# V's weights loaded later, and a scan whose odd bank is given back and written back by ScalarE

## The chip, the cores and the metric

The kernel runs on one core of one Trainium2 chip. The core has TensorE (matrix products into PSUM, eight banks of 512 fp32 columns on 128 partitions), VectorE, ScalarE and GpSimd (elementwise work), and SyncE, here only an issuer of DMA transfers; ScalarE and GpSimd can issue transfers as well. The engines run side by side, each takes its own instructions in program order, and semaphores order them among each other. In the profile PE is TensorE (PEld its weight loads), DVE VectorE, ACT ScalarE, POOL GpSimd, SP SyncE; a q behind a name (SPq, ACTq) means the engine's issues of DMA transfers.

The metric is device time in microseconds of the whole kernel, the median of several runs.

## The reference

Two independent heads over 2048 tokens of width 448; their outputs lie side by side, 896 columns in bf16.

```python
# head A: a diagonal complex state-space scan over all tokens
Lam_bar = exp(dt * Lam);  B_bar = ((Lam_bar - 1) / Lam)[:, None] * Bmat
Bu = x @ B_bar.T                       # complex, 448 states
h[t] = Lam_bar * h[t-1] + Bu[t]
yA = 2 * Re(h @ Cmat.T) + x * Dskip
# head B: local dilated attention, 16 heads of width 28
q, k, v = split(x @ wqkv)
# token s looks at s, s-2, ..., s-14 (8 keys, masked before the start)
yB = (softmax(q . k / sqrt(28)) @ v) @ wo
out = concatenate([yA, yB], axis=-1)
```

## The kernel before

Every piece of work is a unit: a Python closure with the engine that runs it, its dependencies and the PSUM banks that it takes and gives back. `Planner.run` (line 162) emits the units in the order of one hand-kept list of unit numbers, `ORDER` (line 46), and `BANKS` (line 76) says which banks each taking of a slot gets. So the order on every engine and on every queue is fixed by that list; a number from 1000 on means the second engine of a unit that has two to choose from. The costs and priorities written beside the units do not act at run time.

Head B. `loads` (line 322) brings B_x transposed, on SP, into the tile `rb`: the first 1024 tokens in four transfers (line 348), the others in four (line 352). The Q and K columns of `wqkv` come in three groups of columns, the first on ScalarE's queue, the others on SP's (line 359), and are copied between the partition halves by `shift` (line 381, seen as line 201 on ScalarE and 205 on VectorE). `load_v` (line 391) brings V's columns into `wv` in four transfers, lines 336 to 340. `prep` (line 427) projects Q and K: `first` (line 485, matmuls of line 493) for two key tiles of the first 1024 tokens, `proj` (line 438, line 452) for the rest; evictions are copies of line 201 and 203 into `qk`. `dup` (line 531) copies the last key tile to the other partition half with SP. `qk` (line 538) multiplies Q with shifted K on VectorE (line 559) and sums over head columns on TensorE (line 572). `softmax` (line 587), `v_proj` (line 655, matmuls of line 672 reading `wv`) and `pv` (line 709) follow: VectorE multiplies weights with V (line 726), adds (732) and folds (735 to 743), SP turns the folded sums (line 770), TensorE applies `wo` (lines 789 and 796), and copies into `ra` go out by line 806.

Head A. A_x is loaded transposed, sixteen transfers of line 867 and one of 870, into `xaT_sb`. The scan (line 1093) treats 16 consecutive tokens as 4 by 4 steps, and goes over 7 groups of 64 states. In each group TensorE forms the inputs of four steps (line 1134) in banks: "P" holds steps 0 and 2 (two banks), "1" and "3" one each. ScalarE reads "P" into `eP` (line 1147), TensorE adds powers of it to "1" and "3" (line 1151), ScalarE reads "1" into `e1` (line 1155), and so on through "3", a two-level chain of small copies and products over all 128 blocks (lines 1173, 1178, 1184); then `ev3` (line 1187) writes step 3, `s5` (line 1202, matmuls of 1190 and 1191) adds the carry to "1" and `ev1f` reads step 1; `s6` and `s7` do the same for "P", and `evPf` reads steps 0 and 2. What happens to a bank between the first reading and the carry is in `FIN`, for "P" and "1" in this order:

```python
FIN = (("seed", "hold"),) * 7
```

"hold" keeps the bank with its sums until the carry is added; "seed" gives it back after the reading and later takes a bank again, into which ScalarE copies the read sums (line 1216 for "P"; `back1`, line 1195, would do it for "1"). `powers` (line 1067) makes the matrices of powers, on VectorE (line 1083) or ScalarE (line 1081).

`outputs` (line 1308) multiplies the states by C (line 1318) for pairs of tokens, adds x times Dskip (matmuls of 1337 for half of the tokens, a ScalarE copy of line 1330 into the bank for the others), copies the sums into `ra` (line 201 on ScalarE, 205 on VectorE) and sends them out on SP (line 1341). The last three pairs are copied and sent one token at a time.

Of the kernel before, what the change touches and what calls it, by code (L numbers as in the profile page):

```python
# [9 lines left out]
ACT = mybir.ActivationFunctionType  # L10
# [6 lines left out]
D = 448  # L17
# [22 lines left out]
NHO = 4  # L40
NF = 3
WARM = (7, 4)
FIN = (("seed", "hold"),) * 7
PES = (0, 1)
PRI = dict(bm=-5.66, xa=2.77, cc=19.9, sc=2.9, ch=-27.35, bk=-0.56, v0=16.0, v1=-26.16, wo=-13.74, y=14.16, pw=-5.68, sm=13.48, lim=100.0, lim2=30.0, limv=70.0, qk=0.86, K11=-14.0, Q11=-13.0, K10=-12.0, Q10=-11.0, K01=-10.0, Q01=-9.0, K00=-8.0, Q00=-7.0, d3=10.94, h0=-1.0, g0=-1.0, h1=-1.0, g1=-1.0, h2=-1.0, g2=-1.0, h3=1.0, g3=-1.0, h4=-1.0, g4=-1.0, h5=-1.0, g5=-1.0, h6=1.0, g6=1.0, nd=4.0, xd=20.12)
ORDER = [
# [28 lines left out]
]  # L75
BANKS = [
    0, 0, 2, 3, 5, 0, 2, 4, 6, 2, 4, 0, 6, 4, 2, 0, 2, 4, 0, 2, 4, 0, 4, 6, 7, 0, 2, 6, 0, 7, 6, 2, 0, 1, 2, 4,
    5, 2, 5, 4, 7, 5, 2, 2, 5, 3, 2, 0, 0, 6, 5, 4, 6, 0, 3, 2, 6, 0, 6, 0, 1, 6, 4, 6, 4, 2, 6, 2, 0, 2, 6, 0,
    4, 2, 6, 0, 4, 2,
]  # L80
TWO_PI = 2.0 * math.pi
MAGIC = 12582912.0
# [2 lines left out]
def pe(n, cols):  # L85
    return n * (cols / 2400.0 + 0.003)


def act(n):
    return n / 1200.0 + 0.055  # L90


def vec(n):
    return n / 960.0 + 0.07
# [26 lines left out]
class Planner:  # L121
# [6 lines left out]
    def add(self, eng, cost, fn, deps=(), prio=0.0, acq=None, rel=None, lat=None, until=None,  # L128
            mode="f", kind=None, dma=0.0):
        u = Unit()  # L130
        u.mode, u.kind, u.dma = mode, kind, dma
        u.eng = eng if isinstance(eng, tuple) else (eng,)
        u.cost = cost if isinstance(cost, tuple) else (cost,)
        u.fn, u.prio, u.until = fn, prio, until
        u.acq, u.rel = [() if v is None else tuple(v) if isinstance(v, (tuple, list)) else (v,) for v in (acq, rel)]
        u.lat = {"PE": 0.275, "ACT": 0.22, "DVE": 0.27}.get(u.eng[0], 0.15) if lat is None else lat
        u.deps = [d for d in deps if d is not None]
        u.end, u.seq, u.on = None, len(self.units), None
        self.units.append(u)
        return u  # L140
# [171 lines left out]
class PartB:  # L312
# [396 lines left out]
    def pv(self, b, prio, deps):  # L709
# [8 lines left out]
        for r in range(2):  # L718
# [27 lines left out]
            for x in (0, 1):  # L746
                o = 4 * r + 8 * x
                dd = [self.u_vh[b, p] if p < HALO else self.u_v[b, p - HALO] for p in range(o, o + 10)]
                ms.append(P.add("DVE", vec2(4 * n1), lambda x=x, f=mul: f(x), [*dd, *after, last], prio + 0.1 * r))
            last = P.add("DVE", vec2(4 * n1) + 0.11, add, ms, prio + 0.1 * r)  # L750
            if g < 3:
                last = P.add("DVE", vec2(2 * n1) + vec2(n1) + 0.2, fold, [last, *self.u_proj, self.u_trd.get(g - 2)], prio + 0.1 * r)
# [71 lines left out]
class PartA:  # L824
# [268 lines left out]
    def scan(self, prio, qk_done):  # L1093
# [8 lines left out]
        for m in range(NM):  # L1102
# [8 lines left out]
            def hget(m=m):  # L1111
                if m not in self.h:
# [7 lines left out]
            sl = {"P": Slot("B", 2, 0, 2), 1: Slot("B", 2), 3: Slot("B", 2), "fl": Slot("fl"),  # L1120
                  "P2": Slot("B", 2, 2 if FIN[m][0] == "seed" else 0, 2), "b1": Slot("B", 2, 2 if FIN[m][1] == "seed" else 0)}
            begun = set()
# [69 lines left out]

            mP, m1 = FIN[m]

# [113 lines left out]
    def outputs(self, prio):  # L1308
        nc, pool, P, cx = self.nc, self.pool, self.plan, self.cx
        for n, j in enumerate(range(0, T, 2)):  # L1310
            pr = prio + n / 100
            jb = {}
# [5 lines left out]
                    nc.tensor.matmul(ps, lhsT=self.h[m][:, i, g * NCH:(g + 1) * NCH], rhs=self.Ccat[:, m, :],  # L1318
                                     start=False, stop=(m == NM - 1), skip_group_check=True)

            def ev(eng, j=j, jb=jb, j0=0, j1=2):
                cx.late_tile()
                if j0 == 0:
                    jb["r"] = cx.ya_ring.get()
                o = cx.ya_v[:, jb["r"], j0:j1]
                cx.copy(eng, o, jb["y"][:, j0:j1, 0:D])

            def seed(j=j, jb=jb):
                jb["y"] = self.psum.tile([NCH, 2, 512], f32, name="y_ps", slot=jb["s"])
# [14 lines left out]
            sl = jb["s"] = Slot("B", 1, 0 if j // 4 in PES else 1, 2)  # L1344
            pc = pe(7, 448)
            hs = [self.u_h[:20], self.u_h[20:24], self.u_h[24:]]
            if j // 4 in PES:
                first = [P.add("PE", pe(4, 112), lambda f=skip, i=i: f(i), [self.u_dg, self.u_x[j], self.u_x[j + 1], *self.u_xx.values()],
                               pr, acq=sl) for i in range(2)]
# [3 lines left out]
            if n < 3:  # L1353
                pc -= pe(2, 448)
                us = [P.add("PE", pc, lambda f=y, i=i: f(i, m1=5), hs[0] + self.u_cc + first, pr, acq=sl) for i in range(2)]
                v = P.add("PE", pe(2, 448), lambda f=y: (f(0, m0=5, m1=6), f(1, m0=5, m1=6)), us + hs[1], pr)
                v = P.add("PE", pe(2, 448), lambda f=y: (f(0, m0=6), f(1, m0=6)), [v] + hs[2], pr)
                us = [v, v]
            else:
                us = [P.add("PE", pc, lambda f=y, i=i: f(i), self.u_h + self.u_cc + first, pr, acq=sl) for i in range(2)]  # L1360
            en = lambda n: (("ACT", "DVE"), (act(n) + 0.13 * (n > 512), vec(n)))
            e = lambda f, **k: (lambda eng: f(eng, **k))
            if n < 5:
                v = P.add(*en(896), e(ev), us + x + cx.u_free, pr - 2, rel=sl, acq="ya")
                P.add("SP", 0.45, out, [v], pr, rel="ya", lat=1.1, dma=1.0)
            else:
                u = P.add(*en(448), e(ev, j0=0, j1=1), us[:1] + x + cx.u_free, pr - 2, acq="ya")
                o = P.add("SP", 0.45, lambda f=out: f(j0=0, j1=1), [u], pr, lat=1.1, dma=0.5)
                v = P.add(*en(448), e(ev, j0=1, j1=2), [us[1], u], pr - 2, rel=sl)
                P.add("SP", 0.45, lambda f=out: f(j0=1, j1=2), [v, o], pr, rel="ya", lat=1.1, dma=0.5)  # L1370


@with_exitstack
def kernel(
# [36 lines left out]
    cx = Ctx(tc, pool, _Ps(), plan)  # L1411
    cx.dram = ctx.enter_context(tc.tile_pool(name="dram", bufs=1, space=bass.MemoryType.DRAM))
    b = PartB(cx, B_x, B_wqkv, B_wo, out[0].rearrange("(b p j) e -> b p j e", b=2, j=JB)[:, :, :, D:2 * D])
# [14 lines left out]
    cx.consts2()  # L1428
    b.prep(u_warm)
    a.load_x([b.u0])  # L1430
    b.load_v([b.u0])
    a.setup_weights(PRI["bm"])
    cx.u_bm = a.u_bm
    b.load_wo(a.u_bm)
# [42 lines left out]
```

## Time and profile before

| | us |
|---|---|
| three runs | 137.06, 136.56, 135.93 (median 136.56) |
| the profiled execution | 136.07 |
| its span, first to last instruction | 134.4 |
| TensorE busy in the span | 126.9 |
| VectorE busy | 113.8 |
| ScalarE busy | 103.4 |
| mean granted TensorE clock | 1.00 |

The profile is that of one execution. Busy time is the time in which an engine had at least one instruction running; matmuls are pipelined and their ends are modelled, so a busy TensorE can still wait. The chain that ended last is followed back from the last instruction: at each step to what released it, or to the instruction before it on its engine. A row of a timeline gives the start, the duration, the engine, the line, what is written from what, and in brackets how long the engine stood idle before it and what ended that. A row of a group gives line, engine, operation, output from input, shapes, count, then busy microseconds, mean nanoseconds of one, and idle time before.

### The profile page before, as it was taken

To read this page: it belongs to the slowest core of one execution; us is meant where nothing else is said; L and a number is where in the kernel's file an instruction comes from. 1 tells how busy PE (TensorE), PEld (TensorE's weight loads), DVE (VectorE), ACT (ScalarE), POOL (GpSimd) and SP (SyncE) were. 2 spreads that over 40 slices of the span, in tenths; PEclk is the share of its full clock that TensorE was granted. 3 is DMA by queue.
4 is the path that set the end of the run, shared out by engine and by line. 5 is a ranking of instruction groups with operands and counts; after the bars stand their busy time and mean duration, and the time that the engine had idled before them with its cause. 6 is when DMAs were issued, how large, how long until landed. Compare 5 with 4: busy or idle time off the path is not lost.

```text
span 134.4 us, 2479 instructions
## 1 busy us (share of the span) xinstructions
PE 126.9 (94%) x921; PEld 63.5 (47%) x921; DVE 113.8 (85%) x131; ACT 103.4 (77%) x189; POOL 9.7 (7%) x28
## 2 busy tenths in 40 slices
PE   6968999999999999999999899999999999999990
PEld 2445544433546344564544445454556555455440
DVE  5215999999999999999999999999999999991120
ACT  2027999999899987797789998988979737877141
POOL 6940070000000000000000000000000000000000
PEclk9999999999999999999999999999999999999999
DMA  4999999473854749855558989125810630459543
GB/s 101 238 270 225 170 165 211 104 151 84 92 124 99 197 95 282 207 122 126 148 129 137 242 211 250 61 67 138 231 49 0 153 121 0 143 172 262 187 145 120
DMA packets 47759, 20.25 MB, mean 151 GB/s; under 512 B 38774, under 2 KB 46346, under 8 KB 47748
## 3 DMA queue, kind: packets, MB, share of 16 engines
q1 hardware_dynamic: 45716, 18.96, 61.6%
q10 hardware_dynamic: 1840, 1.11, 3.3%
q8 instruction: 7, 0.11, 0.3%
q0 software_dynamic: 192, 0.03, 0.1%
q14 instruction: 4, 0.03, 0.1%
HBM read 5.18 MB, written 4.19 MB: 70 GB/s over the span
## 4 chain that ended last, share of the span: by engine, by line
PE 82%; ACT 6%; DMA 4%; SPq 4%; issue 1%; ACTq 0%
PE banks L1318 15%; PE banks L1134 15%; PE banks L452 12%; PE banks L672 8%; PE banks L789 7%; PE banks L572 6%; DMA rb<-in_B_x_dram 4%; PE banks L1178 3%; SPq L348 3%; PE banks L493 2%; PE banks L1151 2%; PE banks L796 2%; PE banks L1191 2%; ACT eP L1147 1%; ACT pbuf L1173 1%
## 5 line engine op out<-in xcount | busy, mean ns | idle before, releaser
L559 DVE TENSOR_TENSOR prods<-qk 128x4096 bf16<-128x4096 bf16 (+1 forms) x18 | 31.8, 1810 | 0.2
L1134 PE MATMUL banks<-xaT_sb,Bcat 128*128 128x512 bf16 (+1 forms) x112 | 26.7, 382 | 0.0
L201 ACT CAST ra<-banks 128x896 bf16<-128x896 f32 (+2 forms) x22 | 16.9, 802 | 8.6 <-PE banks L1318 5.2
L201 ACT CAST qk<-banks 128x512 bf16<-128x512 f32 (+3 forms) x20 | 16.9, 846 | 1.6 <-PE banks L1191 1.2
L732 DVE TENSOR_TENSOR prods<-prods 128x7168 bf16<-128x7168 bf16 x4 | 15.6, 3891 | 0.1
L726 DVE TENSOR_TENSOR prods<-ra 128x7168 bf16<-128x7168 bf16 x4 | 15.5, 3886 | 0.1
L726 DVE TENSOR_TENSOR prods<-ra,qk 128x7168 bf16<-128x7168 bf16 x4 | 15.5, 3886 | 0.0
L1318 PE MATMUL banks<-Ccat,h 128*128 128x448 bf16 x64 | 14.8, 354 | 0.0
L452 PE MATMUL banks<-rb 128*128 128x512 bf16 (+1 forms) x64 | 14.0, 380 | 0.0
L1134 PEld LDWEIGHTS <-Bcat 128*128 128x128 bf16 (+1 forms) x112 | 9.0, 100 | 10.5 <-issue 4.0
L672 PE MATMUL banks<-wv,rb 128*128 128x448 bf16 (+1 forms) x64 | 13.4, 354 | 0.0
L1173 ACT CAST pbuf<-banks 128x64 bf16<-128x64 f32 (+1 forms) x42 | 9.5, 233 | 3.8 <-PE banks L1178 2.9
L1318 PE MATMUL banks<-Ccat,qk 128*128 128x448 bf16 x48 | 11.7, 352 | 0.0
L789 PE MATMUL banks<-wo_p,rb 128*128 128x448 bf16 x48 | 10.5, 354 | 0.0
L1178 PE MATMUL banks<-pbuf,pw 128*128 128x64 bf16 x77 | 10.1, 235 | 0.3 <-ACT pbuf L1173 0.3
L493 PE MATMUL banks<-rb 128*128 128x256 bf16 (+2 forms) x76 | 7.9, 256 | 1.8 <-DMA rb<-in_B_x_dram 0.6
L1178 PEld LDWEIGHTS <-pw 128*128 128x128 bf16 x77 | 6.4, 105 | 5.9 <-issue 1.6
L203 ACT ACTIVATE qk<-banks 128x512 bf16<-128x512 f32 (+2 forms) x10 | 8.5, 850 | 0.2
L1318 PEld LDWEIGHTS <-h 128*128 128x128 bf16 x64 | 5.9, 99 | 5.5 <-issue 0.9
L452 PEld LDWEIGHTS <-rb 128*128 128x128 bf16 (+1 forms) x64 | 5.0, 97 | 7.1 <-issue 2.5
L1147 ACT CAST eP<-banks 128x1024 bf16<-128x1024 f32 x7 | 7.2, 1023 | 1.5 <-PE banks L1134 1.5
L201 ACT CAST h<-banks 128x512 bf16<-128x512 f32 (+1 forms) x8 | 6.5, 808 | 1.9 <-PE banks L1191 1.8
(145 smaller groups left out, 191.8 us busy)
## 6 DMA issues: line engine op xcount, KB each, us to landing
out_dram<-ra SPq DMA_DIRECT2D x12, 224.0 KB, 2.4
xaT_sb<-in_A_x_dram SPq DMA_DIRECT2D x2, 448.0 KB, 4.1
out_dram<-ra SPq DMA_DIRECT2D x8, 112.0 KB, 1.7
ra<-ra SPq DMA_DIRECT2D x2, 392.0 KB, 4.4
qk<-qk SPq DMA_DIRECT2D x2, 392.0 KB, 3.7
wv<-in_B_wqkv_dram ACTq DMA_DIRECT2D x2, 336.0 KB, 5.2
ra<-ra SPq DMA_DIRECT2D x1, 588.0 KB
qk<-qk SPq DMA_DIRECT2D x1, 588.0 KB, 5.0
```

The costliest lines, as they stand in the source:

```text
L201: nc.scalar.copy(out, in_)
L452: nc.tensor.matmul(out(e)[:, j0:j1], lhsT=w, rhs=self.xB[rows, b, j0:j1, c, :], start=e not in begun, stop=True, skip_group_check=True)
L493: nc.tensor.matmul(box["ps"][:, e, k, 64 * j0:64 * j1], lhsT=self.wqk[rows, c, D * k + NCH * kt:D * k + NCH * kt + NCH], rhs=self.xB[rows, ...
L559: V.tensor_tensor(p[:, :, a:a + n], q[:, t0 + a:t0 + a + n].unsqueeze(1).to_broadcast([NCH, 4, n]), bass.AP(k.tensor, k.offset, [k.ap[0], ...
L672: nc.tensor.matmul(box["ps"][:, e, 0:D], lhsT=self.xB[rows, b, jj, c, :], rhs=self.wv[rows, c, :], start=e not in begun, stop=True, skip_g ...
L726: V.tensor_tensor(out.rearrange("p (u i d h) -> p u i d h", u=4, i=4, d=DH), self.attn[b][:, r].rearrange("p (x u i) h -> p x u i h", x=2, ...
L732: V.tensor_tensor(T1, T1, T2, op=ALU.add)
L789: nc.tensor.matmul(ps, lhsT=o[:, kt + x, :], rhs=self.wo_p[:, (KT + 1) * x + kt, :], start=(kt == 0), stop=False, skip_group_check=True)
L1134: mt(ps(i), lhsT=lhsT, rhs=rhs, start=i not in begun, stop=True, **kw)
L1173: nc.scalar.copy(pb[:, dst, PAD:PAD + NCH // d], tot(a, d))
L1178: mt(tot(out, 2), lhsT=L(T * unit * k), rhs=pb[:, src, PAD - sh:PAD - sh + NCH // 2], start=False, stop=True, **kw)
L1318: nc.tensor.matmul(ps, lhsT=self.h[m][:, i, g * NCH:(g + 1) * NCH], rhs=self.Ccat[:, m, :], start=False, stop=(m == NM - 1), skip_group_ch ...
```

## The change

1. V's weights: the unit of `load_v` depends on the eviction of the third key tile of the first 1024 tokens in place of the start marker, and the order runs it on SP, after all B_x loads, seven A_x loads, the load of B and the first `dup`. Before, it was run on ScalarE's queue at the start.
2. The scan: "1" is treated as "seed" too. Its bank is given back after `ev1`, and `back1` on ScalarE (a copy of 128x512 from `e1` into a newly taken bank) comes in for each of the seven groups, seven new units.
3. The last output pair: the copy of its second token is cut in two, columns 0 to 255 on ScalarE and 256 to 447 on VectorE, and the bank is given back after the transfer.
4. The numbers in `ORDER` and `BANKS` are new throughout. What changes in substance: A_x's loads come in another order (the load of B stands after the first three of them, the second `dup` after the last); the first powers of group 0 are made on VectorE, no longer on ScalarE; one of the copies of the first softmax weights goes from VectorE to ScalarE; TensorE's sequence of scan products, V projections and output products is of the same kind with many neighbours exchanged; the last TensorE units are the second tokens of pairs 12 and 14, before it was 10 and 12. The constants in `Planner.add` differ, but act on nothing at run time.

```diff
-FIN = (("seed", "hold"),) * 7
+FIN = (("seed", "seed"),) * 7
 ORDER = [
-    0, 1, 23, 3, 2, 5, 6, 15, 7, 8, 9, 10, 4, 41, 39, 16, 40, 44, 46, 42, 47, 43, 13, 24, 45, 57, 59, 11, 14,
-    12, 21, 1134, 1017, 18, 58, 60, 25, 61, 54, 53, 51, 27, 52, 50, 28, 22, 29, 20, 48, 49, 65, 149, 64, 67, 62,
+    22, 2, 5, 0, 1, 6, 23, 7, 1017, 4, 8, 3, 9, 39, 15, 41, 16, 40, 18, 44, 46, 43, 42, 45, 24, 25, 27, 28, 10,
+    20, 59, 57, 47, 48, 49, 29, 152, 61, 58, 60, 62, 63, 158, 1019, 38, 30, 11, 52, 13, 50, 51, 66, 53, 64, 54,
...
 BANKS = [
...
-        u.lat = {"PE": 0.275, "ACT": 0.22, "DVE": 0.27}.get(u.eng[0], 0.15) if lat is None else lat
+        u.lat = {"PE": 0.285, "ACT": 0.225, "DVE": 0.27}.get(u.eng[0], 0.15) if lat is None else lat
...
-            def ev(eng, j=j, jb=jb, j0=0, j1=2):
+            def ev(eng, j=j, jb=jb, j0=0, j1=2, c0=0, c1=D):
                 cx.late_tile()
                 if j0 == 0:
                     jb["r"] = cx.ya_ring.get()
-                o = cx.ya_v[:, jb["r"], j0:j1]
-                cx.copy(eng, o, jb["y"][:, j0:j1, 0:D])
+                o = cx.ya_v[:, jb["r"], j0:j1, c0:c1]
+                cx.copy(eng, o, jb["y"][:, j0:j1, c0:c1])
...
-                v = P.add(*en(448), e(ev, j0=1, j1=2), [us[1], u], pr - 2, rel=sl)
-                P.add("SP", 0.45, lambda f=out: f(j0=1, j1=2), [v, o], pr, rel="ya", lat=1.1, dma=0.5)
+                if n < 7:
+                    v = [P.add(*en(448), e(ev, j0=1, j1=2), [us[1], u], pr - 2, rel=sl)]
+                else:
+                    v = [P.add("ACT", act(256), lambda f=ev: f("ACT", j0=1, j1=2, c1=256), [us[1], u], pr - 2),
+                         P.add("DVE", vec(192), lambda f=ev: f("DVE", j0=1, j1=2, c0=256), [us[1], u], pr - 2)]
+                P.add("SP", 0.45, lambda f=out: f(j0=1, j1=2), [*v, o], pr, rel=("ya", sl) if n == 7 else "ya", lat=1.1, dma=0.5)
...
-    b.load_v([b.u0])
+    b.load_v([b.u_k[0, 2][-1]])
```

More of the change, by code (lines that the diff above doesn't have):

```diff
@@ L46 @@
 ORDER = [
[28 rows of a table removed]
[29 rows of a table added]
 ]
 BANKS = [
-    0, 0, 2, 3, 5, 0, 2, 4, 6, 2, 4, 0, 6, 4, 2, 0, 2, 4, 0, 2, 4, 0, 4, 6, 7, 0, 2, 6, 0, 7, 6, 2, 0, 1, 2, 4,
-    5, 2, 5, 4, 7, 5, 2, 2, 5, 3, 2, 0, 0, 6, 5, 4, 6, 0, 3, 2, 6, 0, 6, 0, 1, 6, 4, 6, 4, 2, 6, 2, 0, 2, 6, 0,
-    4, 2, 6, 0, 4, 2,
[3 rows of a table added]
 ]
```

56 rows, old and new, of tables (BANKS, ORDER) are left out of this document.

## The prediction

> **What bounds the kernel now.** I read the page's span and chain shares first, then the chain in order of time, then the stretches of the scan.
>
> ```profile
> span 134.4 us, 2479 instructions
> ...
> PE 82%; ACT 6%; DMA 4%; SPq 4%; issue 1%; ACTq 0%
> ```
>
> ```profile
> 6.02 5.75 DMA rb<-in_B_x_dram
> 11.81 3.12 PE banks L493 x28
> ...
> 131.04 0.53 ACT ra L201
> ```
>
> TensorE's own work carries 82% of the chain that ended last (PE in the second row). What is not TensorE's lies in three places: the start, where a transfer of B_x holds the chain until 11.8 us and TensorE runs on from there; pieces of ScalarE inside the scan; and the end, where TensorE's last product is read at 131.04 and stored, and the span closes 3.3 us later. The profiled execution took 136.07 us, 1.7 more than its span, and the sum is made against it; the median of the three runs shown is 136.56, so 0.49 is added at the end.
>
> VectorE matters as much. In the next rows, stretches of ten microseconds, the second figure is TensorE's busy time, the fourth VectorE's, the fifth ScalarE's, and the 1.00 the granted clock:
>
> ```profile
> 60.00:70.00 10.00, 9.76 (x64) 4.76 (x62) 9.93 (x4) 7.88 (x16) 0.00 (x0) 1.00 0.57 139
> 70.00:80.00 10.00, 9.59 (x65) 4.68 (x63) 9.97 (x6) 9.67 (x19) 0.00 (x0) 1.00 0.91 185
> 80.00:90.00 10.00, 10.00 (x68) 4.88 (x68) 9.93 (x9) 8.96 (x21) 0.00 (x0) 1.00 0.47 124
> 90.00:100.00 10.00, 9.66 (x67) 4.89 (x65) 9.96 (x3) 8.72 (x21) 0.00 (x0) 1.00 0.60 161
> 100.00:110.00 10.00, 9.92 (x84) 6.13 (x83) 9.93 (x6) 7.19 (x13) 0.00 (x0) 1.00 0.34 92
> ```
>
> TensorE and VectorE are both full through the scan, and VectorE stays full from its first product (second row below) to its last sum (third row):
>
> ```profile
> 13.04 0.55 DVE L205 COPY rb<-rb 64x1536 bf16<-64x1536 bf16 x1 [1.06 <-DMA rb<-in_B_wqkv_dram]
> 13.62 1.23 DVE L559 TENSOR_TENSOR prods<-qk 128x2048 bf16<-128x2048 bf16 x1
> ...
> 120.13 0.62 DVE L743 TENSOR_TENSOR rb<-prods 128x896 bf16<-128x896 bf16 x1
> ```
>
> That last sum, turned by a transfer, feeds TensorE's last output matmuls. So the end moves if both engines start earlier, or if both lose less time between.
>
> **Part 1: V's weights leave the start.** Before, ScalarE's queue brings them while SP's queue brings B_x and the Q and K columns. The two queues from 6 to 9 us (q1 is SP's, q10 ScalarE's):
>
> ```profile
> q1 hardware_dynamic: 1728, 0.43, 77.5%
> q10 hardware_dynamic: 461, 0.38, 39.6%
> ```
>
> Together they take over 100% of the 16 engines' time, 40 of it V's. The B_x transfers issued then, and those issued after:
>
> ```profile
> L348 SPq DMA_TRANSPOSE rb<-in_B_x_dram x4: 1291/1311/1762, 0.8 to 6.0; - x4
> ...
> DMA to landing us min/median/max: 5.7/5.7/5.7
> ```
>
> ```profile
> L352 SPq DMA_TRANSPOSE rb<-in_B_x_dram x4: 1227/1296/1297, 10.4 to 14.4; - x4
> ...
> DMA to landing us min/median/max: 3.8/4.1/4.3
> ```
>
> A transfer landed 5.7 us after its issue beside V and 4.1 without it, and the slowest issue took 1762 ns against a median of 1311. So the transfer that releases TensorE at 11.81 lands 5.7 - 4.1 = 1.6 us earlier, and up to 0.45 more if its issue is not held back. VectorE's start has the same cause: the row of 13.04 shows it waiting for the last Q and K columns, which SP queues behind those B_x transfers, and its first product follows at 13.62. I take **-1.6 us** for both engines, by the landing alone; the ends are 0 (the transfers limited by their own issue of 1.3 us each) and -2.05.
>
> What it costs later: the four V transfers now stand on SP, behind the B_x loads, seven A_x loads, the load of B and the first copy of the upper key half. Queued behind them on SP are nine A_x loads and the second such copy, and the scan's groups wait for A_x.
>
> ```profile
> wv<-in_B_wqkv_dram ACTq DMA_DIRECT2D x2, 336.0 KB, 5.2
> ```
>
> ```profile
> L867 SPq DMA_TRANSPOSE xaT_sb<-in_A_x_dram x15: 1257/1265/1735, 19.1 to 42.4; - x15
> ```
>
> ```profile
> 38.57 1.78 PE L1134 MATMUL banks<-xaT_sb,Bcat 128*128 128x512 bf16 x8
> ```
>
> SP's A_x loads end at 43.7 now (42.4 and the last issue). They begin up to 1.6 us earlier and carry four issues more, some 0.4 to 0.5 each, so they end about where they did, while the scan's first group (38.57) is wanted 1.6 earlier, near 37. Its first step, A_x's j=0, is the fifth load behind V: counting 1.3 us for each issue from a first B_x load at 9, V is issued near 27 to 28.5 and j=0 near 34, so j=0 is there with a microsecond or less to spare. V, at 5.2 us from issue to landing, arrives near 33, where TensorE's new order first reads it (about 32.5, old place of that matmul less 1.6). I put the loss at 0, with 1 us as the other end: both covers are thin.
>
> **Part 2: the odd bank is given back and written back.** Seven ScalarE copies of 128x512 bf16 into a bank come in, one for each group of the scan; TensorE's count stays the same. The trace has no such copy. The nearest rows:
>
> ```profile
> L1216 ACT CAST banks<-eP 128x1024 f32<-128x1024 bf16 x7 | 7.2, 1034 | 0.0
> ...
> L1330 ACT CAST banks<-xaT_sb 128x896 f32<-128x896 bf16 x4 | 3.6, 914 | 0.9 <-DVE xaT_sb L1304 0.8
> ```
>
> 128 columns less cost 120 ns, so 512 columns cost 1034 - 4 x 120 = 554 ns, and seven 3.9 us. ScalarE's idle time in the five stretches is 50 - 42.4 = 7.6 us. By the new order the first two copies fall in 60:70 (2.1 us idle), the third in 70:80 (0.3 idle), the others where 1.0, 1.3 and 2.8 are idle. What the order takes from ScalarE instead, group 0's first powers, goes near 45 us, where TensorE sets the pace, and costs VectorE this:
>
> ```profile
> L1083 DVE TENSOR_TENSOR pw<-Dm,spair 128x640 bf16<-128x640 bf16 x5 | 2.4, 486 | 0.0
> ```
>
> VectorE gives up a small copy for it, so about 0.2 us is added to its dense work; I count that as hidden, since its last sum is turned and waiting when TensorE comes to it, and at 0.2 if that cover goes.
>
> What is bought is a bank for some ten microseconds of each group, so that TensorE can put another product where it now waits. How much waits there:
>
> ```profile
> 91.52 1.01 ACT eP L1147
> ...
> 94.14 0.49 ACT qk L1187
> ```
>
> From 91.5 to 94.6 the chain runs over ScalarE alone, but TensorE's visible idle time in all five stretches is only 50 - 48.94 = 1.1 us. Its new order of units is close to the old one, so I expect little: the third copy is not absorbed (0.55), about 0.25 comes back: **+0.3**. The ends are -1.1, all of the visible idle time, and +3.9, no copy absorbed.
>
> TensorE's runs of half-height pairs fall from 25 to 23 in the new order.
>
> ```profile
> 98.08 0.29 PE banks L796 x2
> ...
> 127.77 0.48 PE banks L796 x4
> ```
>
> Two pairs cost 0.48 together and 0.58 apart, so 0.1 for each merging, **-0.2**; nothing if the mergings fall in a wait.
>
> **Part 3: the last output is read by two engines.** ScalarE takes 256 columns and VectorE the other 192 of the same bank, and SP's last transfer waits for both.
>
> ```profile
> L201 ACT CAST ra<-banks 128x256 bf16<-128x256 f32 x1 | 0.4, 393 | 0.0
> ```
>
> ```profile
> 128.10 1.62 ACT L201 CAST ra<-banks 128x448 bf16<-128x448 f32 x3 [1.99 <-PE banks L796]
> 128.19 0.36 DVE L205 CAST ra<-banks 128x192 bf16<-128x192 f32 x1 [3.30 <-PE banks L796]
> ```
>
> Side by side they take 0.39 in place of the 0.53 of 131.04: -0.14. One after the other they take 0.39 + 0.36 = 0.75, and something to hand over: about +0.25. The only two pieces of one bank in this trace are these: the 192 columns end at 128.55, and the 256, the third of ScalarE's copies from 128.10, begin near 129.3. They do not overlap, so I take **+0.25**. The Trainium skill, PSUM — Partial Sum Buffer, section "PSUM bank collisions raise a hardware error", speaks against this edit: no two engines may access one bank and quadrant at once, reads included, and the compiler's scheduler puts a dependency between them. By that rule the sum holds +0.25, without it -0.14; the two rows agree with the rule and do not prove it.
>
> **The sum.** -1.6 + 0.3 - 0.2 + 0.25 = -1.25: 134.8 for the profiled execution, 135.3 for the median. About 1%, 1.37 us, is what a measurement of this kernel can tell from no change.
>
> **The rivals.** *The bank pays.* All of TensorE's visible idle time in the scan goes and some of what the pipelined ends hide, 1.5 us beyond the forecast: 133.8. For it speak the ScalarE pieces on the chain; against it, TensorE's little-changed order.
>
> *The start's gain is lost again.* V or A_x lands up to 1 us after TensorE wants it, or the B_x transfers were limited by their own issue and the edit does not do what it says: 136.3 to 136.9. For it speak the thin covers of part 1; against it, 5.7 against 4.1 us.
>
> *ScalarE becomes the bound of the scan, and the kernel slower.* The five copies from 70 us on, 2.75 us, are not absorbed, because an engine that runs in order is idle only while it waits for TensorE: 135.3 - 0.3 + 2.75 = 137.8, and with all seven 138.9. For it speaks 9.67 of 10 us busy in 70:80; against it, the 5.5 us idle from 70 to 110. It decides once ScalarE is over 97% busy from 70 to 105.
>
> **How the numbers follow.** Forecast 0.46, its own range 134.6 to 136.0, with 0.22 past 1%; the bank pays 0.20; the start's gain lost 0.18; ScalarE binds 0.16. Faster 0.22 + 0.20 = 0.42, within 1% 0.24 + 0.18 = 0.42, slower 0.16. The range of 133.6 to 137.4 takes in the second and third case and reaches towards the fourth, leaving out most of it.
>
> **What would show it.** Part 1: L348's landing near 4 us, TensorE's dense run from about 10.2, VectorE's first product near 12.0, SP's A_x loads over near 44. Part 2: seven copies of 512 columns near 0.55 us each, ScalarE above 90% from 60 to 110, no longer stretches of ScalarE on the chain. Part 3: VectorE's 192 columns after ScalarE's 256. The forecast is wrong if TensorE waits for V's weights or A_x between 30 and 46, if VectorE goes idle between its products, or if ScalarE's share of the chain passes 10%.

## The result, and the profile after

| | us |
|---|---|
| before, 20 runs | 136.56 median (135.93 to 137.99) |
| changed, 20 runs | 135.95 median (135.03 to 137.98) |
| ratio | 0.9933, 95% interval 0.991 to 0.9956 |
| changed again, on another occasion, 12 runs | 135.71 median, before 137.05; ratio 0.9896, interval 0.986 to 0.9932 |
| profiled execution | 135.03, span 133.3 (before 136.07, span 134.4) |

The change made the kernel about 0.7 to 1.0% faster; the forecast was 0.9% (135.3). The medians are of all runs, while each ratio leaves out runs more than 1.5% above the fastest of their kernel, so it is not exactly the quotient of the medians. The page of the changed kernel, its span and its chain's shares:

```profile
span 133.3 us, 2479 instructions
...
PE 73%; ACT 15%; SPq 5%; DMA 3%; issue 1%; DVE 0%; ACTq 0%
```

TensorE's own share of the chain fell from 82 to 73%, and ScalarE's rose from 6 to 15%. (The lines of the changed kernel that are shown here stand 1 later than before.) First the start: the two sets of B_x transfers, and the timelines of TensorE and of VectorE.

```profile
L349 SPq DMA_TRANSPOSE rb<-in_B_x_dram x4: 1250/1294/1319, 0.8 to 6.1; - x4
...
DMA to landing us min/median/max: 3.8/4.1/4.4
```

```profile
L353 SPq DMA_TRANSPOSE rb<-in_B_x_dram x4: 1221/1296/1302, 8.6 to 12.6; - x4
...
DMA to landing us min/median/max: 4.0/4.4/5.0
```

```profile
7.72 5.68 PE L494 MATMUL banks<-rb 128*128 128x256 bf16 x52
13.23 3.29 PE L453 MATMUL banks<-rb 128*128 128x512 bf16 x16
17.17 3.09 PE L453 MATMUL banks<-rb 64*128 64x512 bf16 x15 [0.65 <-ACT sh L960]
```

```profile
12.25 2.36 DVE L560 TENSOR_TENSOR prods<-qk 128x2048 bf16<-128x2048 bf16 x2
```

The same place before, and two later ones in the chain of before that are needed below:

```profile
14.76 2.43 PE L452 MATMUL banks<-rb 128*128 128x512 bf16 x11
```

```profile
34.98 1.29 PE banks L452 x6
...
38.73 1.62 PE banks L1134 x8
...
128.25 2.77 PE banks L1318 x14
```

The first B_x transfers land 4.1 us after their issue, 5.7 before, as forecast (the landings count only those transfers whose landing the profile tells, here two of the first four and three of the others, before one of the first four); TensorE reaches the long projections at 13.23, where it was 14.76, and VectorE's first product comes at 12.25 in place of 13.62. But at 17.17 stands an idle time of 0.65 that was not there. The bracket names ScalarE's `sh`, which has nothing to do with these matmuls: they are the first on the second half of B_x. Its last transfer was issued at 12.59 and landed 4.44 later, at 17.03, and the weight load ahead of these matmuls waits for the semaphore of that transfer. The second execution of the same kernel, by its timeline, names the transfer, and the view of line 353 its landing:

```profile
18.17 2.01 PE L453 MATMUL banks<-rb 64*128 64x512 bf16 x10 [1.80 <-DMA rb<-in_B_x_dram]
```

```profile
DMA to landing us min/median/max: 4.0/5.4/6.1
```

There the landings took up to 6.1, that of the last transfer 5.41, and TensorE stood 1.80. The chain of the two executions, first then second, at the places that matter: the first matmuls on the second half of B_x (shown for the second execution), the inputs of the scan's group 0 (x8), a row of the same line in a later group (x3), and the last output matmuls (x14):

```profile
37.81 1.62 PE banks L1135 x8
...
51.82 0.75 PE banks L1135 x3
...
126.98 2.77 PE banks L1319 x14
```

```profile
12.62 5.41 DMA rb<-in_B_x_dram
18.17 5.35 PE banks L453 x28
...
38.80 1.62 PE banks L1135 x8
...
128.00 2.77 PE banks L1319 x14
```

From the wait's end to the last outputs are 109.81 us in the one (17.17 to 126.98) and 109.83 in the other (18.17 to 128.00). So in these two executions the end follows the arrival of B_x's second half at the same distance, and how long that landing takes is why the first is 1.1 us below the kernel before in span and the second (134.3) level with it. That an earlier arrival would bring the end forward as far is not shown by this; a run below, in which TensorE does not wait there, tells more. The scan, by stretches of 10 us, columns as in the prediction:

```profile
60.00:70.00 10.00, 10.00 (x69) 4.89 (x68) 9.90 (x4) 9.81 (x21) 0.00 (x0) 1.00 0.72 172
70.00:80.00 10.00, 9.30 (x60) 4.24 (x58) 9.97 (x7) 9.86 (x21) 0.00 (x0) 1.00 0.98 204
80.00:90.00 10.00, 9.98 (x71) 4.91 (x70) 9.97 (x7) 9.32 (x21) 0.00 (x0) 1.00 0.32 88
90.00:100.00 10.00, 9.87 (x78) 5.51 (x77) 9.96 (x3) 9.80 (x24) 0.00 (x0) 1.00 0.48 117
```

ScalarE is 97% busy from 60 to 100 (38.79 of 40), where it had 35.23 before. The chain runs over it for ten microseconds on end:

```profile
64.86 1.01 ACT h L202
...
74.77 0.81 PE banks L1135 x3
```

The new copies, in the groups of the profile:

```profile
L1199 ACT CAST banks<-e 128x512 f32<-128x512 bf16 x7 | 4.2, 601 | 0.0
```

And yet TensorE's way from group 0's inputs to the last outputs is 89.17 us (89.20 in the second execution); before it was 128.25 - 38.73 = 89.52, so the scan is 0.35 and 0.32 shorter. The end of the changed kernel:

```profile
129.77 0.37 ACT L202 CAST ra<-banks 128x256 bf16<-128x256 f32 x1 [0.79 <-PE banks L1319]
130.18 0.36 DVE L206 CAST ra<-banks 128x192 bf16<-128x192 f32 x1 [1.34 <-ACT ra L202]
130.56 0.33 SPq L1342 DMA_DIRECT2D out_dram<-ra  x1
```

VectorE's 192 columns wait for ScalarE's 256, and the bracket says so.

### The profile page after: what moved, and what is told of

The parts are those of the page before. It is cut to its first block, busy times and chain, and to the rows that moved or that the text cites. A ratio compares the mean times of both kernels' runs of the same rounds, so it can differ in the third digit from the quotient of the medians.

```text
span 133.3 us, 2479 instructions
## 1 busy us (share of the span) xinstructions
PE 126.8 (95%) x921; PEld 63.4 (48%) x921; DVE 113.4 (85%) x130; ACT 105.4 (79%) x189; POOL 12.1 (9%) x28
## 4 chain that ended last, share of the span: by engine, by line
PE 73%; ACT 15%; SPq 5%; DMA 3%; issue 1%; DVE 0%; ACTq 0%
PE banks L1319 16%; PE banks L1135 12%; PE banks L453 10%; PE banks L790 7%; PE banks L673 7%; PE banks L573 6%; SPq L349 4%; PE banks L1179 3%; DMA rb<-in_B_wqkv_dram 3%; ACT qk L202 2%; ACT pbuf L1174 2%; PE banks L1152 2%; ACT h L202 2%; PE banks L797 2%; ACT banks L1217 1%; SPq L360 1%
## 5 line engine op out<-in xcount | busy, mean ns | idle before, releaser
L202 ACT CAST ra<-banks 128x896 bf16<-128x896 f32 (+2 forms) x24 | 17.9, 773 | 7.8 <-PE banks L797 4.2
L453 PE MATMUL banks<-rb 128*128 128x512 bf16 (+1 forms) x64 | 13.3, 379 | 0.6 <-ACT sh L960 0.6
L206 DVE CAST ra<-banks 128x192 bf16<-128x192 f32 x2 | 0.7, 358 | 9.2 <-ACT ra L202 9.2
L1084 DVE TENSOR_TENSOR pw<-Dm,spair 128x1280 bf16<-128x1280 bf16 (+1 forms) x13 | 8.0, 664 | 0.0
```

Source lines behind the costliest of these rows:

```text
L202: nc.scalar.copy(out, in_)
L453: nc.tensor.matmul(out(e)[:, j0:j1], lhsT=w, rhs=self.xB[rows, b, j0:j1, c, :], start=e not in begun, stop=True, skip_group_check=True)
```

## The experiments

**The base.** The changed kernel unaltered.

> The changed kernel once more, unaltered, as the base of the three others. Both theories: 135.9 us median (ratio to before 0.993). Theory 'start': the changed kernel owes its gain to the earlier start (TensorE runs on from 7.7 us, VectorE's first product at 12.25, 1.4 earlier than before) and pays 0.65 us at 17 us, where TensorE waits for the second half of B_x, and 0.23 at the tail. Theory 'scan': most of the start's lead is lost before the scan begins, and what is left comes from the freed bank. Its trace shall show again the 0.65 us wait at 17 us, and how much a second profiled execution differs from the first (span 133.3).

135.71 us, ratio 0.9896 (0.986 to 0.9932); its trace is the second execution above. The wait was there again and longer, 1.80.

**V back at the start.** `changed` with V on ScalarE's queue:

```diff
-    22, 2, 5, 0, 1, 6, 23, 7, 1017, 4, 8, 3,
+    22, 2, 5, 0, 1, 6, 23, 7, 1134, 1017, 4, 8, 3,
...
-    84, 165, 88, 134, 95,
+    84, 165, 88, 95,
...
-    b.load_v([b.u_k[0, 2][-1]])
+    b.load_v([b.u0])
```

> The changed kernel with V's weights back on ScalarE's queue at the start; everything else, the freed bank too, as changed. Theory 'start': the first matmul run goes back by 1.4 to 1.6 us and the 0.65 us wait at 17 us goes away: 136.7 to 137.3 us, slower than before. Theory 'scan': 136.0 to 136.4, still faster than before.

137.99 us, ratio 1.0043 (1.0004 to 1.0081): 1.5% above the changed kernel on the same occasion, a little slower than before. The landing of the first B_x transfers, and its chain:

```profile
DMA to landing us min/median/max: 5.9/5.9/5.9
```

```profile
14.51 4.65 DMA rb<-in_B_x_dram
19.40 5.35 PE banks L453 x28
...
129.21 2.77 PE banks L1319 x14
```

The first landing (the profile tells one of the four) is 5.9 again, the last transfer of the second half is issued at 14.51 in place of 12.62 and lands 4.65 later, and from the first matmuls on it to the last outputs are the same 109.81. So the start's gain is real and belongs to V; the new order without it would be a loss. I had expected the wait of 17 us to go; it stayed, since the second half is late with the first.

**V late alone, twice.** The kernel before with V on SP, behind the B_x transfers:

```diff
-    12, 21, 1134, 1017, 18, 58,
+    12, 134, 21, 1017, 18, 58,
```

> The kernel before with one edit: V's weights are issued on SP right behind the eight B_x transfers, no longer on ScalarE's queue at the start; the scan, the tail and the rest of the order as before. Theory 'start': the B_x transfers land near 4 us after their issue, TensorE's dense run begins 1.6 us earlier, and it keeps 1.0 to 1.6 of it: 135.0 to 135.6 us, ratio near 0.99. Theory 'scan': the lead is lost in the middle, 136.2 to 136.6, ratio 0.997 to 1.0. Rival, B_x limited by its own issue: landing stays near 5.7 us and the time at 136.5.

136.84 us, ratio 1.0 (0.9962 to 1.0037). TensorE's timeline has the lead, the chain shows where it went:

```profile
12.75 2.43 PE L452 MATMUL banks<-rb 128*128 128x512 bf16 x11
```

```profile
26.75 2.64 DMA qk<-qk
...
31.71 2.29 DVE prods L559
34.83 1.29 PE banks L452 x6
```

TensorE was at its long projections at 12.75, 2.0 earlier than before, but at 34.83 it stands where it stood before (34.98): SP's queue of transposes, 1.3 us each and with V's issues now among them, brought the copy of the upper key half (`qk<-qk`) too late for VectorE. Then with V behind that copy, as the changed kernel has it, and the V projection of 26 us moved to 42:

```diff
-    12, 21, 1134, 1017, 18, 58,
+    12, 21, 1017, 18, 58,
...
-    151, 154, 158, 159, 160, 105, 309, 33, 92, 215, 214, 88, 97,
+    151, 154, 158, 159, 160, 105, 309, 33, 92, 88, 97,
...
-    162, 99, 84, 108, 95,
+    162, 99, 84, 134, 108, 95,
...
-    146, 210, 178,
+    146, 215, 214, 216, 217, 210, 178,
```

(units 216 and 217, the rest of that projection and its eviction, leave their old places too; the bank taken is 0.)

> The kernel before with V's weights on SP behind the first copy of the upper key half, as the changed kernel has them, and the V projection that stood at 26 us moved to 42 us on TensorE, since V lands near 31; the scan with its held bank, and the tail, as before. Theory 'start': the product that waited for that copy in the first such test (31.7 us) is early again, and the start's 1.6 us stay: 135.0 to 135.4, ratio 0.988 to 0.991. Theory 'the lead runs into something else in the old order': 136.2 to 136.8, ratio 0.997 to 1.0, and its trace shows a new wait between 20 and 60 us.

138.26 us, ratio 1.0065 (1.0031 to 1.0098): slower. Of its waits from 12 to 62 us, the one of group 0's matmuls (1.8 us, once):

```profile
PE banks L1134 <- DMA xaT_sb<-in_A_x_dram: 1.8, 1, 1.8
```

Now A_x is late: V's four issues stand in SP's queue ahead of six A_x loads, the last of which group 0 waits for. In neither of the two places tried does V's later load pay with the rest of the old order; in the changed kernel, where it does, the order of A_x is another too. What of the new order it needs was not separated. That SP's queue is a path of its own, both runs show.

**The wait at 17.** `changed` with M, the projection of the last key tile of the first half, ahead of the first projections of the second:

```diff
-    37, 129, 26, 107, 91, 89, 106, 117, 90, 105, 35, 79, 74, 121, 80, 81, 87, 21, 92, 99, 108, 151, 160, 154, 98, 82,
+    37, 129, 26, 79, 80, 81, 107, 106, 105, 117, 35, 74, 82, 83, 91, 89, 90, 87, 108, 92, 151, 160, 154, 99, 121, 21, 98,
```

> The changed kernel with the projection of the last key tile's first 1024 tokens (unit M, eight matmuls, 1.6 us) put ahead of the first projections of the other 1024 tokens, its two evictions ahead of theirs, and the sums of the first products a little earlier; banks of these units permuted, all else as changed. Theory 'second half of B_x': TensorE's path after that transfer lands is fixed at 109.8 us (from 17.17 to 126.98 in one profiled execution, from 18.17 to 128.00 in another), so M fills a wait of 0.65 to 1.8 us: 134.3 to 135.0 us, ratio 0.980 to 0.986 to before, and the executions spread less. Theory 'VectorE sets the path': VectorE's products and sums stay where they are, and the time stays at 135.7 (ratio 0.990).

135.27 us, ratio 0.9904 (0.9866 to 0.9942): no better than the base. With the last copy whole as well:

> The same with the last output copy whole on ScalarE: 0.2 less than the kernel with M first alone, 134.1 to 134.8 if the wait for B_x's second half is the cause, 135.5 if not.

135.47 us, ratio 0.9917 (0.9877 to 0.9957), no better either. TensorE's timeline of the first, and VectorE's of both:

```profile
16.47 1.79 PE L453 MATMUL banks<-rb,wm 128*128 128x512 bf16 x8
18.10 3.83 PE L453 MATMUL banks<-rb 64*128 64x512 bf16 x18
```

```profile
47.20 4.49 DVE L560 TENSOR_TENSOR prods<-qk 128x4096 bf16<-128x4096 bf16 x2 [1.18 <-DMA qk<-qk]
```

```profile
46.39 4.49 DVE L560 TENSOR_TENSOR prods<-qk 128x4096 bf16<-128x4096 bf16 x2 [0.44 <-DMA qk<-qk]
```

The wait is gone, M fills it. In its place VectorE waits 1.18 and 0.44 for the second copy of the upper key half, which SP issues behind all A_x loads; the chain of the first runs over SP's issues to that copy, here the copy itself:

```profile
44.31 2.76 DMA qk<-qk
```

In its profiled execution the second kernel has group 0's inputs at 37.46, where the changed kernel had them at 37.81 and 38.80, so some of TensorE's lead got that far; its span was 132.8, the shortest of all. In the medians of both nothing of it is to be seen, and one execution does not show that filling the wait is worth anything.

**SP's end, two attempts.** V issued by ScalarE at 24 us, where it waits for TensorE:

```diff
-    127, 36, 33, 94, 120,
+    127, 36, 33, 1134, 94, 120,
...
-    84, 165, 88, 134, 95,
+    84, 165, 88, 95,
```

> The kernel with M first and the last copy whole, and V's four transfers issued by ScalarE at 24 us, where it waits for TensorE, in place of SP at 26 us. In the run with M first VectorE stood idle 1.18 us at 47 us, and in the one with the whole last copy 0.44 us, for the second copy of the upper key half, which SP issues behind all A_x loads; without V's four issues (2.4 us) that copy goes out at about 41 in place of 43 to 44. Theory 'three queues': that idle time goes, ScalarE pays up to 0.5 for the issues, and the slower executions come down: 134.5 to 134.9 us, ratio 0.982 to 0.985. Rival, TensorE alone sets the end and the copy is covered: 135.3, ratio 0.990.

149.04 us, ratio 1.0888 (1.0835 to 1.0941), a miss by 14 us:

```profile
38.29 1.02 ACT L204 ACTIVATE qk<-banks 128x1024 bf16<-128x1024 f32 x1 [13.05 <-DMA wv<-in_B_wqkv_dram]
```

```profile
32.08 3.94 DMA xaT_sb<-in_A_x_dram
...
36.04 2.27 DMA wv<-in_B_wqkv_dram
```

ScalarE was free at 25.2 and got its first issue out at 30.9 and the last before 38.3. In the trace the landings of SP's and ScalarE's transfers are counted by eight counters (semaphores) that the transfers of both queues take in turn, and each of these issues waits for the transfer that had its counter before. Those were A_x loads that SP reached only later: the second issue went out at 36.04, as soon as the A_x load that SP had issued at 32.08 had landed (36.02). In the edited list these loads stand behind V; why they come ahead of it in the counters' turn was not found. So this run says nothing on whether SP's queue is relieved by taking V from it.

The other attempt puts the second copy ahead of the last A_x load:

```diff
-    131, 210, 171, 1378, 146, 212, 178, 114,
+    114, 131, 210, 171, 1378, 146, 212, 178,
```

> The kernel with M first and the last copy whole, and SP's second copy of the upper key half put ahead of the last A_x load (two issues of 1.25 and 0.59 us) in place of behind it. It goes out near 41.5 in place of 43.1 to 43.7, so VectorE's idle time of 0.44 to 1.18 us at 46 to 47 us goes; the last A_x load lands 1.2 later, for whose rest a ScalarE copy at 46.2 waits, with about 0.2 to 0.5 to lose. Theory 'three queues': the executions that were held by that copy come down to those held by TensorE alone, 134.5 to 135.0 us, ratio 0.982 to 0.987. Rival, that idle time is covered by TensorE's own work in most executions: 135.3, ratio 0.990.

135.76 us against 137.61 before in the same runs, ratio 0.9871 (0.9809 to 0.9934). VectorE's idle time is gone, and a new wait is in the list, for the load that now stands last:

```profile
ACT xaT_sb L202 <- DMA xaT_sb<-xa_rest: 1.3, 1, 1.3
```

The ratio is the lowest of all, but its interval holds that of the base; that it beats the changed kernel isn't shown.

**The tail.** `changed` with `if n < 8` in place of `if n < 7`, so that the last copy is one of 448 columns on ScalarE.

> The changed kernel with its last output copy whole on ScalarE (448 columns), as before the change, in place of 256 on ScalarE and 192 on VectorE. Taken as the two pieces run one after the other, 0.77 us against 0.53: 0.23 faster than the changed kernel, near 135.7. If two engines had overlapped it would be 0.14 slower, near 136.1.

135.37 us, ratio 0.9885 (0.9842 to 0.9929), too near the base to be told from it; the trace tells it:

```profile
130.71 0.53 ACT L202 CAST ra<-banks 128x448 bf16<-128x448 f32 x1 [0.79 <-PE banks L1319]
131.27 0.33 SPq L1342 DMA_DIRECT2D out_dram<-ra  x1
```

```profile
127.92 2.77 PE banks L1319 x14
```

From the last matmuls' start, the second row, to the last issue are 3.35 us; with the split they are 130.56 - 126.98 = 3.58. The split costs 0.23.

**The price of the write-back.** Three kernels change only `back1`: one lets TensorE do it, one copies twice, one copies 128 columns of 512.

```diff
-FIN = (("seed", "seed"),) * 7
+FIN = (("seed", "pe"),) * 7
```

> The changed kernel with its seven write-backs of the odd bank done by TensorE (identity times e1, one matmul of 512 columns each, 7 x 0.21 = 1.5 us) in place of ScalarE's seven copies (7 x 0.55 = 3.9 us). If ScalarE's order binds the scan, as the chain of the changed kernel from 65 to 75 us says: 134.5 to 135.3, faster than changed. If TensorE's count binds it: 1.0 to 1.5 slower than changed, 136.7 to 137.2.

138.66 us, ratio 1.0109 (1.0048 to 1.017): 1.8 to 2.2% above the base in ratio, more than TensorE's 1.5 us. Why it is more stays open; no trace of it here can be compared.

```diff
                     nc.scalar.copy(box[1], box["e1"][:])
+                    nc.scalar.copy(box[1], box["e1"][:])
```

> The changed kernel with every write-back of the odd bank copied twice by ScalarE, 3.9 us more of its work. If ScalarE's spare time takes the copies in: 135.7 to 136.2, at most 0.5 above changed. If ScalarE binds: 1.5 to 3.9 above changed, 137.2 to 139.6; half of that is then what the copies cost in the changed kernel.

138.81 us, ratio 1.0152 (1.0105 to 1.0198). Its second copies, and in its chain the first matmuls on the second half of B_x, the row in the later group and the last outputs (one line later):

```profile
L1200 ACT CAST banks<-e 128x512 f32<-128x512 bf16 x7 | 4.1, 590 | 0.2
```

```profile
17.33 5.35 PE banks L453 x28
...
51.98 0.75 PE banks L1135 x3
...
129.88 2.77 PE banks L1320 x14
```

From 17.33 to 129.88 are 112.55, 2.74 more than 109.81: two thirds of 4.1 us of copies come through. From the row in the later group they are 77.90, where the changed kernel has 126.98 - 51.82 = 75.16: all of the 2.74 arises there.

```diff
-                    nc.scalar.copy(box[1], box["e1"][:])
+                    nc.scalar.copy(box[1][:, 0:NCH], box["e1"][:, 0:NCH])
```

> The changed kernel with only the first 128 of the 512 columns of e1 written back to the odd bank; the rest of the bank is left as it is, so the states of the odd tokens are not computed in full. ScalarE's seven copies fall from 0.55 to about 0.23 us, 2.2 us less of its work; all else as changed. If ScalarE binds the scan as the doubled copies suggest (3.1 us for 3.9): 1.7 us faster than changed, 134.0. If the copies lie in its spare time or beside VectorE's work: 135.4 to 135.9. Half of 1.7 would say that the first of two copies costs less than the second.

135.98 us against 137.16, ratio 0.9904 (0.9867 to 0.9941): level with the base. The 1.7 us that a bound ScalarE would have given back (ratio 0.977 to 0.981) are outside the interval; a few tenths are not. Its chain tells more, as the same stretch leaves out what its start lost:

```profile
53.85 0.75 PE banks L1135 x3
...
128.91 2.77 PE banks L1319 x14
```

That is 75.06, against 75.16: with its copies down from 4.2 us to 2.0, TensorE's way is 0.10 shorter.

So taking half of the first copy's time away gains next to nothing, while a second copy is far from free. Why is not shown: the second copy may bind because ScalarE has no more room, or because it hands the bank to the next matmuls later; the runs do not separate the two.

## Why the prediction was right, and where it was not

The forecast of 135.3 lies between the two measurements, taken in ratio (0.9908 against 0.9933 and 0.9896). By its steps:

- **Part 1, -1.6 for both engines.** The lead at the front came as worked out: landing 4.1 for 5.7, no issue above 1319 ns, TensorE at the long projections 14.76 - 13.23 = 1.53 earlier, VectorE's product 1.37. V and A_x came in time in the changed order; the rival that they would not showed where the old order of A_x was kept, and for one load where the key copy was put ahead of it. What failed is the sentence that TensorE runs on from there: at group 0's inputs it is 38.73 - 37.81 = 0.92 ahead in one execution and 0.07 behind in the other. I had used the second half of B_x only as a measure of a landing without V beside it, and not asked when TensorE's new order wants it. It starts 1.8 earlier than before (8.6 for 10.4), but the new order asks for it ahead of M, and the landing of its last transfer took 4.4 and 5.4 where the median before had been 4.1. With M in front TensorE no longer waits there, and the next wait is close behind: VectorE's for the second key copy. So the term is -0.9 to 0, not -1.6; the end 0 of its range was reached, and with it, by another way than I had named, the rival *the start's gain is lost again*.
- **Part 2, +0.3, and the mergings, -0.2.** Together +0.1; measured from group 0's inputs to the last outputs -0.35 and -0.32. The seven copies took 601 ns each (I had 554), 4.2 us in all, and cost next to nothing; two marks that I had set spoke for the opposite. ScalarE's long stretches on the chain did not shorten: from 64.86 to 74.77 the chain is nearly ScalarE alone, and its share of 15% passes the 10% that were to prove the forecast wrong. A share of the chain says who came last, not how close behind the next one was. The altered copies say that: 2.2 us less of them moves 0.10, 4.1 more moves 2.74. The rival *ScalarE becomes the bound* put its point at over 97% busy from 70 to 105; the changed kernel has 94.9 and 97.0% there in its two profiled executions, the doubled copy 98.1%. How much of the -0.35 is the freed bank, how much the mergings and how much the other exchanges of the new order was not separated; no run has the freed bank alone.
- **Part 3, +0.25.** 0.23, one after the other as the two rows of the trace before had it. The rule of the Trainium skill, PSUM — Partial Sum Buffer, section "PSUM bank collisions raise a hardware error", speaks of a dependency between the two reads; the trace agrees, VectorE's copy begins 0.41 after the start of ScalarE's, which takes 0.37. What two reads at once would do, no run here shows.
- **The sum.** -0.92 - 0.35 + 0.23 = -1.04 for the first profiled execution (135.03 for 136.07, -1.04 measured) and +0.07 - 0.32 + 0.23 = -0.02 for the second, which took 136.04 (-0.03). That the forecast was right in size is in part luck: a gain in the scan that I had not counted stood in for part of the start's that was lost, and in the second execution, where all of the start's was lost, only a few hundredths are left of the gain.

## What to carry to other kernels

When a change starts an engine earlier, go through every queue that feeds it, and work out for each when its next transfer is wanted by the new order and when it lands at best; a queue whose issues take 1.3 us each is an engine with a path of its own, here as long as TensorE's from the first microsecond to the 44th. A load that slows others can be moved to a later place, but then look at the queue that it joins: the wait may come back there. Whether an engine that is 97% busy binds is not read from its share: make its work a little more and a little less, and see which of the two moves the time.

## What the runs showed of the hardware that was not expected

- Four transposing loads, issued at the same times to 0.1 us, landed after 4.0/4.4/5.0 us (minimum, median, maximum) in one execution of the changed kernel and after 4.0/5.4/6.1 in another; issued 1.9 later, with V at the start, the two whose landing the profile tells took 3.8, and the last, by the chain, 4.65. What slows them was not found.
- An issue of ScalarE's queue can wait for loads of SP's queue, through counters that the two share: in one run ScalarE stood 13.05 us behind such issues, and one of them went out at 36.04, when the load of SP's that had its counter before had landed at 36.02.
